# A fused adaLN block, forward and backward: the MLP's inner gradient and its modulated rows transposed from SBUF to SBUF, the filter gradient formed in place

## The chip, the core and the metric

The kernel runs on one core of a Trainium2 chip, in one launch. A core has five instruction queues: TensorE (PE, with its weight loads shown apart as PEld), VectorE (DVE), ScalarE (ACT), GpSimd (POOL) and SyncE (SP). In this kernel SP computes nothing: it issues DMAs, in the order of its queue, and waits in place when the DMA at its head has to wait. The metric is device time in microseconds (us), lower is better; three timed runs of the kernel before gave 420.84, 421.02 and 421.93 us, a median of 421.02 us.

## What is computed

The reference is a forward pass and its vector-Jacobian product. `x` is 2048 rows of 512 channels (S = 2048, D = 512), the MLP has F = 1792 inner channels, everything in bf16:

```python
mod = silu(c) @ w_mod                       # six rows of 512: sa, ca, ga, sb, cb, gb
h = layernorm(x) * (1 + ca) + sa
x = x + ga * irfft2(rfft2(h) * (w_r + 1j * w_i))   # spectral mixing over rows and channels
h = layernorm(x) * (1 + cb) + sb
x = x + gb * (relu(h @ w1 + b1) ** 2 @ w2 + b2)
# outputs: x, and for a given grad_out the gradients of
# A_x, A_w_r, A_w_i, B_w1, B_b1, B_w2, B_b2, c, w_mod
```

Two intermediate quantities matter here. The *modulated rows* are the second `h`, called h2 in the kernel: the MLP's input. The *inner gradient*, gh, is the gradient at the MLP's hidden layer before the ReLU. Then grad w1 = h2ᵀ · gh (a sum over the 2048 rows) and grad b1 is the column sum of gh. For both, TensorE needs gh with rows on the 128 partitions; the kernel produces it with inner channels on the partitions. That is why it has to be transposed. The *filter gradient* is the gradient of w_r and w_i: a complex product of the kept forward spectrum X with the gradient's spectrum G.

## The kernel before

The 2048 rows are 16 tiles of 128 (NT = 16), handled in four batches of four tiles (NB = 4, 512 rows each). The 1792 inner channels are 14 chunks of 128 (NFC = 14). The program is written with a tile framework: pools give out buffers, the framework adds every semaphore wait that a read or a reuse of a buffer needs, and its scheduler orders the instructions of each engine by priorities and its own estimates of durations. [...]

The work goes through these stages:

1. Start: loads, modulation rows, first layer norm, first spectral stage, and `back_products` (line 707), which computes grad_out·w2ᵀ into `gaT[b]`, 14 chunks of [128 channels, 512 rows] per batch. The four `gaT` tiles are a ring of four buffers named `gab` (line 546).
2. The spectral product, forward (`spec_f23`, `spec_g1`).
3. The four batches (line 1025). For batch b, `stage_h(b)` (line 872) computes the hidden layer in pairs of chunks: `r` = ReLU (ACT), `h2` = r·r into a ring of seven buffers, and gh = r·gaT in place in `gaT[b]` (DVE). It stores h to DRAM (line 895) and gh to DRAM (line 896). `stage_o(b)` (line 967) is the MLP's second product, `stage_gn(b)` (line 917) multiplies gh by w1ᵀ and goes back through the layer norm. `stage_m(b+1)` (line 830) forms the modulated rows `h2r`, stores them to DRAM (line 838), and reads them back transposed into `h2T` (line 842), the input of the next `stage_h`. Beside batch 3, `f1_again` (line 997) reloads the gradient rows of batches 0 and 1 from DRAM into tiles named x and y (line 1003) and scales them on DVE (line 1008).
4. `ghn_part(b, fc)` (line 865) reads gh of a finished batch back from DRAM, transposed, two chunks at a time: seven DMAs of 256 KB per batch, into a buffer of the `gab` ring. For batches 0 to 2 these are emitted beside the following batch's `stage_gn`, for batch 3 beside `stage_o(3)`.
5. The backward spectral stage (line 1167): for eight groups, `cmul` forms the product with Z, and with X into `gW` (line 1184), which is stored. Z and X come back from DRAM (lines 1173, 1175; X in a ring of four buffers). Between these, TensorE works off 16 units of `grad_w1` (line 1140), each 16 matmuls of [128, 448], and one `grad_b1` (line 1093): 64 matmuls with 32 output columns, in four column groups of the array that take 448 columns each.
6. The end: the rows' backward pass (`row_pair`, `row_end`) merged with `grad_w2` (line 1224), then the gradient of the modulation.

SP carries nearly all DMAs: the trace has 298 on its queue, 62 of them transposes. Each of its DMAs also waits until the DMA eight places before it has landed, where that is not known from another wait, since eight semaphores are used in turn.

The transposed read of stage 4 is one statement:

```python
nc.sync.dma_start(ghn[b][:, :, fc * P:(fc + 2) * P],
    gh_dram[fc * P:(fc + 2) * P, b * SB:(b + 1) * SB], transpose=True)   # L870
```

## Time and profile before

| what | value |
|---|---|
| median of three timed runs | 421.02 us |
| span of the profiled execution, first to last instruction | 416.3 us |
| what lies around the span, against that median | 4.7 us |
| memory traffic over the span | 35.44 MB read from HBM, 41.60 MB written |
| DMA packets under 512 B | 99049 of 143923 |

The profiled execution's own total is not listed apart from its span, so the difference to the median of the timed runs stands for what lies around it. Two more answers of the trace give the DMAs that the change touches:

| DMA | number | time on SP each (min/median/max) | issue to landing (min/median/max) |
|---|---|---|---|
| store of gh, L896 | 28 | 0.372 / 0.514 / 1.094 us | 3.0 / 3.6 / 5.1 us |
| transposed load of gh, L870 | 28 | 1.277 / 1.309 / 6.002 us | 3.2 / 3.9 / 5.6 us |
| store of the modulated rows, L838 | 8 | 0.332 / 0.344 / 0.349 us | 2.1 / 2.1 / 2.3 us |
| transposed load of the modulated rows, L842 | 6 | 1.237 / 1.238 / 2.003 us | 3.3 / 3.3 / 4.1 us |

"Time on SP" is how long the issuing instruction occupies the queue; "landing" is when the data's semaphore is complete. [...]

### The profile page before, as it was taken

How to read it: one execution, taken by the hardware profiler on the slowest of the kernel's cores; microseconds unless marked ns; L12 is line 12 of the kernel's file. 1: busy time of each engine (PE TensorE's matmuls, PEld its weight loads, DVE VectorE, ACT ScalarE, POOL GpSimd, SP SyncE). 2: the span in 40 equal slices, each digit the busy share in tenths (PEclk: the TensorE clock that was granted, in tenths of full speed). 3: DMA queues.
4: the chain of work that ended last, by engine and by line, in shares of the span. 5: the costliest groups of instructions: out<-in, count | busy, mean ns of one | idle time of the engine just before them, and what ended most of it. 6: DMA issues, size and time to landing. Idle time of an engine off the chain costs nothing. (4 is left out here: it accounts for less than half of the span.)

```text
span 416.3 us, 7175 instructions
## 1 busy us (share of the span) xinstructions
PE 391.7 (94%) x2387; PEld 197.6 (47%) x2407; DVE 343.7 (83%) x827; ACT 277.1 (67%) x495; POOL 60.6 (15%) x147
## 2 busy tenths in 40 slices
PE   2789999999899999999999999999999999999996
PEld 0345445664444444444444444445555665444444
DVE  6899868977988578988897998964999784877885
ACT  4568699868884079338924776545655567897785
POOL 7437950000000000000000000001314520000000
PEclk9999999999999999999999999999999999999999
DMA  8999899979199459949976997998999999999994
GB/s 240 232 261 298 237 213 313 323 239 240 40 331 324 126 161 276 248 128 204 288 227 194 201 291 278 291 213 245 287 280 283 350 265 227 223 269 223 239 266 143
DMA packets 143923, 101.11 MB, mean 243 GB/s; under 512 B 99049, under 2 KB 126830, under 8 KB 143630
## 3 DMA queue, kind: packets, MB, share of 16 engines
q1 hardware_dynamic: 140394, 92.96, 84.1%
q0 software_dynamic: 2784, 7.10, 5.6%
q10 hardware_dynamic: 708, 0.59, 0.5%
q8 instruction: 19, 0.31, 0.3%
q14 instruction: 18, 0.15, 0.1%
HBM read 35.44 MB, written 41.60 MB: 185 GB/s over the span
## 5 line engine op out<-in xcount | busy, mean ns | idle before, releaser
L714 PE MATMUL mm<-gT,w2T 128*128 128x512 bf16 x224 | 57.9, 382 | 4.5 <-ACT gab L719 4.2
L1144 PE MATMUL mm<-gab,h_sb 128*128 128x448 bf16 x256 | 50.9, 352 | 0.0
L1232 PE MATMUL mm<-g_sb,hn 128*128 128x512 bf16 (+1 forms) x250 | 49.6, 352 | 0.8 <-ACT gw L1234 0.4
L915 PE MATMUL og<-w1T,gab 128*128 128x512 bf16 x219 | 49.9, 379 | 0.3
L915 PE MATMUL og<-w,h 128*128 128x512 bf16 x216 | 49.1, 379 | 0.4
L886 PE MATMUL mm<-h2T,w 128*128 128x512 bf16 x164 | 40.2, 379 | 0.5 <-ACT r L888 0.3
L1232 PEld LDWEIGHTS <-hn 128*128 128x128 bf16 x256 | 24.4, 98 | 23.4 <-issue 2.0
L1144 PEld LDWEIGHTS <-h_sb 128*128 128x128 bf16 x256 | 24.6, 98 | 21.8 <-issue 0.8
L886 PEld LDWEIGHTS <-w 128*128 128x128 bf16 x224 | 21.3, 98 | 27.7 <-issue 4.9
L915 PEld LDWEIGHTS <-h 128*128 128x128 bf16 x224 | 21.7, 98 | 25.6 <-DVE h L890 0.6
L915 PEld LDWEIGHTS <-gab 128*128 128x128 bf16 x224 | 21.6, 98 | 25.5 <-DVE gab L894 1.0
L714 PEld LDWEIGHTS <-w2T 128*128 128x128 bf16 x224 | 21.2, 98 | 24.2 <-issue 7.9
L888 ACT ACTIVATE r<-mm,b1col 128x512 bf16<-128x512 f32 x41 | 27.4, 688 | 6.3 <-DVE gab L894 3.3
L294 POOL MEMSET AE<- 128x2 bf16 x4 | 0.3, 103 | 188.5 <-DMA gh_dram<-gab 188.5
L928 ACT CAST G<-og 128x512 bf16<-128x512 f32 x16 | 9.2, 580 | 22.2 <-PE og L915 22.2
L329 ACT ACTIVATE AE<-psB 128x1024 bf16<-128x1024 f32 x16 | 21.8, 1363 | 1.8 <-PE psB L324 0.9
L719 ACT CAST gab<-mm 128x512 bf16<-128x512 f32 x36 | 21.0, 593 | 2.6 <-PE mm L714 2.3
L890 DVE TENSOR_TENSOR h<-r 128x1024 bf16<-128x1024 bf16 x28 | 19.2, 686 | 2.6 <-ACT r L888 2.5
L1148 ACT CAST gw<-mm 128x448 bf16<-128x448 f32 x16 | 8.6, 537 | 18.4 <-PE mm L1144 18.4
L477 DVE SCALAR_TENSOR_TENSOR gm_junk<-wmc,onef,gmbc 128x512 bf16<-128x512 bf16 x24 | 18.0, 750 | 3.3 <-ACT gmbc L467 2.2
L894 DVE TENSOR_TENSOR gab<-r,gab 128x1024 bf16<-128x1024 bf16 x28 | 19.2, 684 | 0.0
L379 ACT ACTIVATE Tsb<-psT 128x512 bf16<-128x512 f32 x32 | 18.5, 603 | 0.6 <-ACT utcs L368 0.5
(292 smaller groups left out, 818.5 us busy)
## 6 DMA issues: line engine op xcount, KB each, us to landing
h_dram<-h SPq DMA_DIRECT2D x28, 256.0 KB, 3.2
gh_dram<-gab SPq DMA_DIRECT2D x28, 256.0 KB, 3.6
w<-in_B_w_dram SPq DMA_DIRECT2D x2, 1792.0 KB, 9.0
wmc<-in_w_mod_dram SPq DMA_DIRECT2D x12, 256.0 KB, 5.8
wz_dram<-Z SPq DMA_DIRECT2D x8, 258.0 KB, 3.8
xs_dram<-Xs SPq DMA_DIRECT2D x8, 258.0 KB, 4.0
Z<-wz_dram SPq DMA_DIRECT2D x8, 258.0 KB, 6.0
Xb<-xs_dram SPq DMA_DIRECT2D x8, 258.0 KB, 8.2
```

The lines of the kernel that those rows point to most:

```text
L329: nc.scalar.activation(dst, ps.rearrange("p r (s e f) -> p (r s) e f", s=2, e=2), AF.Copy, scale=EF_S)
L379: K["Tsb"] = nc.scalar.activation(Tsb, ps, AF.Copy, scale=EF_S).ins
L477: nc.vector.scalar_tensor_tensor(out=junk, in0=wmc[:, i, :], scalar=K["onef"], in1=gmbc, op0=ALU.mult, op1=ALU.mult, accum_out=self.gsc[:, ...
L714: nc.tensor.matmul(ps, lhsT=w2T[:, dc, fc * P:(fc + 1) * P], rhs=gT[b][:, :, dc, :], start=(dc == 0), stop=(dc == 3))
L719: nc.scalar.copy(out=gaT[b][:, fc, :], in_=ps)
L886: nc.tensor.matmul(ps, lhsT=w1[:, dc, (fc + i) * P:(fc + i + 1) * P], rhs=h2T[b][:, :, dc, :], start=(dc == 0), stop=(dc == 3))
L888: nc.scalar.activation(r[:, i, :], ps, AF.Relu, bias=b1col[:, fc + i:fc + i + 1])
L890: nc.vector.tensor_tensor(h2, r, r, op=ALU.mult)
L894: K["gh"] = nc.vector.tensor_tensor(gh, r, gh, op=ALU.mult).ins
L915: nc.tensor.matmul(ps, lhsT=lhs(fc), rhs=rhs[:, fc, :], start=(fc == 0), stop=(fc == NFC - 1))
L1144: nc.tensor.matmul(ps[:, 0:W4], lhsT=h2_sb[:, t, dc * P:(dc + 1) * P], rhs=ghn[t // 4][:, t % 4, fs], start=(t == 0), stop=(t == NT - 1))
L1232: nc.tensor.matmul(ps[:, 0:w], lhsT=hns[fc][:, t, :], rhs=g_sb[:, t, c:c + w], start=(t == 0), stop=(t == NT - 1))
```

## The change

The change has five parts.

1. gh is no longer stored to DRAM. The four `gaT` tiles become one tile `gall` of 4·14 + 2 chunk slots, in which `gaT[b]` starts two slots in. `ghn_part` transposes two chunks of `gaT[b]` into the two slots just before them. So the transposed chunks of a batch take the place of the ones transposed before: chunk pair fc writes the slots that pair fc−2 was read from, and must wait until that transpose has landed and until TensorE has read those slots for the last time in `stage_gn(b)`. The seven transposes of a batch form a chain, and the first pair of a batch follows the last pair of the batch before. The slots 0 and 1 hold two small tiles of the start (`scb`, `srow`) before that.
2. The modulated rows are transposed from `h2r` in SBUF. The store to DRAM stays, since h2 is read again later. The buffer `h2r` (there is one) comes free when both the store and the transpose have landed.
3. The transposed gh now lies block by block (chunk, tile, 128 channels), so `grad_w1` and `grad_b1` take whole chunks: blocks of 4, 3, 4 and 3 chunks, 512 or 384 columns, in place of four times 448. `grad_b1` is read from PSUM by four ACT copies and stored by two DMAs.
4. The filter gradient is written over X. `gW` goes, and X has six buffers in place of four.
5. The last sum of the rows' backward pass is written over `gs`, which has three buffers in place of two; `gx` goes. `gcrow` moves to another pool.

```diff
--- before.py
+++ after.py
@@ -495,7 +495,6 @@
     wz_dram = dram.tile([P, 8, 2, 2, FP], BF16, name="wz_dram")
     xs_dram = dram.tile([P, 8, 2, 2, FP], BF16, name="xs_dram")
     h_dram = dram.tile([NFC, P, NT * P], BF16, name="h_dram")
-    gh_dram = dram.tile([F, NT * P], BF16, name="gh_dram")
     Cd_dram = dram.tile([P, D], BF16, name="Cd_dram")
     LF_dram = dram.tile([P, 16, 3, P], BF16, name="LF_dram")
     LG_dram = dram.tile([P, 16, 3, P], BF16, name="LG_dram")
@@ -543,7 +542,9 @@
     cf_dr = iota_cf(tc, gen)
 
     gap = tc.alloc_tile_pool(name="gap", bufs=1)
-    gaT = [gap.tile([P, NFC, SB], BF16, name="gab", bufs=4) for b in range(NB)]
+    SHIFT = 2
+    gall = gap.tile([P, NB * NFC + SHIFT, SB], BF16, name="gab")
+    gaT = [gall[:, SHIFT + NFC * b:SHIFT + NFC * b + NFC, :] for b in range(NB)]
     w2gp = tc.alloc_tile_pool(name="w2gp", bufs=1)
     zp = tc.alloc_tile_pool(name="zp", bufs=1)
     Z = [zp.tile([P, 2, 2, FP], BF16, name=f"Z{gi}") for gi in range(8)]
@@ -588,7 +589,7 @@
         pv = psM.tile([P, 32], BF16, name="vrow_ps", bufs=1)
         nc.tensor.transpose(pv[:, 0:4 + NFC], vrow, K["ident"][0:4 + NFC, 0:4 + NFC])
         sig = nc.scalar.activation(sigcol, pv[:, 0:4], AF.Sigmoid)
-        scb = p0.tile([P, 4, P], BF16, name="scb")
+        scb = gall[:, 0, :].rearrange("p (a q) -> p a q", q=P)
         for dc in range(4):
             nc.scalar.activation(scb[:, dc, :], pv[:, dc:dc + 1].broadcast_to([P, P]), AF.Copy, scale=sigcol[:, dc:dc + 1])
     nc.vector.tensor_copy(b1col, pv[:, 4:4 + NFC])
@@ -596,7 +597,7 @@
     nc.vector.tensor_copy(scf, scb[:, :, 0])
 
 
-    srow = p0.tile([1, D], BF16, name="srow")
+    srow = gall[0:1, 1, :]
 
     def mod_row(j):
         ps = psM.tile([P, D], FP32, name="mod_ps", bufs=1)
@@ -839,7 +840,7 @@
                 if b > 0:
                     if j == 0:
                         h2T[b] = rows.tile([P, TB, 4, P], BF16, name="h2T", bufs=1)
-                    K["h2T"] = nc.sync.dma_start(h2T[b][:, j:j + 2].rearrange("p j c q -> p (j c) q"), h2_dram[:, t:t + 2, :].rearrange("p j d -> p (j d)"),
+                    K["h2T"] = nc.sync.dma_start(h2T[b][:, j:j + 2].rearrange("p j c q -> p (j c) q"), h2r.rearrange("p j d -> p (j d)"),
                                       transpose=True).ins
 
             return [lambda j=j: one(j) for j in (0, 2)]
@@ -865,9 +866,8 @@
         def ghn_part(b, fc):
 
             if fc == 0:
-                tl = gap.tile([P, NFC, SB], BF16, name="gab", bufs=4)
-                ghn[b] = tl.rearrange("p a b -> p (a b)").rearrange("p (j f) -> p j f", f=F)
-            nc.sync.dma_start(ghn[b][:, :, fc * P:(fc + 2) * P], gh_dram[fc * P:(fc + 2) * P, b * SB:(b + 1) * SB], transpose=True)
+                ghn[b] = gall[:, NFC * b:NFC * b + NFC, :].rearrange("p a (j c) -> p a j c", c=P)
+            nc.sync.dma_start(ghn[b][:, fc:fc + 2].rearrange("p a j c -> p (a j) c"), gaT[b][:, fc:fc + 2, :].rearrange("p a s -> p (a s)"), transpose=True)
 
         def stage_h(b, extra, first):
             sl = slice(b * SB, (b + 1) * SB)
@@ -893,7 +893,6 @@
                 gh = gaT[b][:, fc:fc + 2, :]
                 K["gh"] = nc.vector.tensor_tensor(gh, r, gh, op=ALU.mult).ins
                 nc.sync.dma_start(h_dram[fc:fc + 2, :, sl].rearrange("a p s -> p a s"), h2)
-                nc.sync.dma_start(gh_dram[fc * P:(fc + 2) * P, sl].rearrange("(a p) s -> p a s", p=P), gh)
                 if b == 0 and 0 < fc < 10:
                     load_w1T(fc // 2 - 1)
                 if fc in (4, 10):
@@ -1054,7 +1053,7 @@
                 merge(stage_o(b), [x for p in zip([lambda: None] * 3 + [late_f1.flush] + [lambda: None] * 3, parts) for x in p])
         late.flush()
         nc.vector.tensor_copy(grow[0:96, :], acc[0:96, :])
-        gcrow = constp.tile([1, D], BF16, name="gcrow")
+        gcrow = h2p.tile([1, D], BF16, name="gcrow")
         nc.scalar.copy(out=gcrow, in_=acc[96:97, :])
     hring.release()
     rows.release()
@@ -1080,8 +1079,16 @@
     fin = tc.alloc_tile_pool(name="fin", bufs=2, side="right")
     gmp = tc.alloc_tile_pool(name="gmp", bufs=1, side="right")
     K["LF"] += [lf2.tile([P, 2, 3, P], BF16, name=f"LFb{gi}") for gi in range(4, 8)]
-    W4 = 448
-    NFB = F // W4
+    FBS = [(0, 4), (4, 3), (7, 4), (11, 3)]
+    NFB = len(FBS)
+
+    def gh_rows(t, fb):
+        a, n = FBS[fb]
+        return ghn[t // 4][:, a:a + n, t % 4, :]
+
+    def blocks(ps, fb):
+        return ps[..., 0:FBS[fb][1] * P].rearrange("p (a c) -> p a c", c=P)
+
     gwa = tc.alloc_tile_pool(name="gwa", bufs=1)
     lg2 = tc.alloc_tile_pool(name="lg2", bufs=1)
     K["LG"] = lg2.tile([P, 16, 3, P], BF16, name="LGb")
@@ -1095,11 +1102,15 @@
         ps = mmps.tile([P, SB], FP32, name="mm")
         for t in range(NT):
             for fb in range(NFB):
-                nc.tensor.matmul(ps[32 * fb:32 * fb + 32, 0:W4], lhsT=K["ones_q"], rhs=ghn[t // 4][:, t % 4, fb * W4:(fb + 1) * W4],
+                nc.tensor.matmul(blocks(ps[32 * fb:32 * fb + 32, :], fb), lhsT=K["ones_q"], rhs=gh_rows(t, fb),
                                  start=(t == 0), stop=(t == NT - 1), tile_position=(0, 32 * fb))
-        b4 = gmp.tile([P, W4], BF16, name="b4", bufs=1)
-        nc.scalar.copy(out=b4, in_=ps[:, 0:W4])
-        nc.gpsimd.dma_start(out_5.rearrange("(q f) -> q f", q=NFB), b4[0:P:32, :])
+        b4 = gmp.tile([P, SB], BF16, name="b4", bufs=1)
+        for q in range(4):
+            w = FBS[q][1] * P
+            nc.scalar.copy(out=b4[32 * q:32 * q + 32, 0:w], in_=ps[32 * q:32 * q + 32, 0:w])
+        o5 = out_5.rearrange("(h f) -> h f", h=2)
+        nc.gpsimd.dma_start(o5[:, 0:SB], b4[0:P:64, :])
+        nc.gpsimd.dma_start(o5[:, SB:F // 2], b4[32:P:64, 0:F // 2 - SB])
 
     def add_quadrants(ps, pool, out):
         w = ps.shape[-1]
@@ -1138,16 +1149,16 @@
     w1o = {}
 
     def grad_w1(fb, dc):
-        fs = slice(fb * W4, (fb + 1) * W4)
         ps = mmps.tile([P, SB], FP32, name="mm")
         for t in range(NT):
-            nc.tensor.matmul(ps[:, 0:W4], lhsT=h2_sb[:, t, dc * P:(dc + 1) * P], rhs=ghn[t // 4][:, t % 4, fs],
-                             start=(t == 0), stop=(t == NT - 1))
+            nc.tensor.matmul(blocks(ps, fb), lhsT=h2_sb[:, t, dc * P:(dc + 1) * P], rhs=gh_rows(t, fb), start=(t == 0), stop=(t == NT - 1))
+        a, n = FBS[fb]
         if fb % 2 == 0:
-            w1o[0] = gwa.tile([P, 2, W4], BF16, name="gw1", bufs=3)
-        nc.scalar.copy(out=w1o[0][:, fb % 2, :], in_=ps[:, 0:W4])
+            w1o[0] = gwa.tile([P, F // 2], BF16, name="gw1", bufs=3)
+        half = SB * (fb % 2)
+        nc.scalar.copy(out=w1o[0][:, half:half + n * P], in_=ps[:, 0:n * P])
         if fb % 2 == 1:
-            nc.gpsimd.dma_start(out4_view[:, dc, (fb - 1) * W4:(fb + 1) * W4], w1o[0].rearrange("p a f -> p (a f)"))
+            nc.gpsimd.dma_start(out4_view[:, dc, (a - 4) * P:(a + n) * P], w1o[0])
 
     units = []
     for fp in range(0, NFB, 2):
@@ -1171,7 +1182,7 @@
             if gi >= 4:
                 nc.sync.dma_start(K["LF"][gi], LF_dram[:, 2 * gi:2 * gi + 2])
             nc.sync.dma_start(Z[gi], wz_dram[:, gi])
-            Xt[gi] = fr.tile([P, 2, 2, FP], BF16, name="Xb", bufs=4)
+            Xt[gi] = fr.tile([P, 2, 2, FP], BF16, name="Xb", bufs=6)
             nc.sync.dma_start(Xt[gi], xs_dram[:, gi])
 
         for gi in range(4):
@@ -1181,8 +1192,8 @@
 
         def ew_b(gi, G):
             cmul(nc, ew, Z[gi], G, Z[gi][:, :, 0, 0:DF], Z[gi][:, :, 1, 0:DF], True)
-            gW = ew.tile([P, 2, 2, FP], BF16, name="gW", bufs=3)
-            cmul(nc, ew, Xt[gi], G, gW[:, 0, :, 0:DF], gW[:, 1, :, 0:DF], True)
+            gW = Xt[gi].rearrange("p h i f -> p i h f")
+            cmul(nc, ew, Xt[gi], G, Xt[gi][:, :, 0, 0:DF], Xt[gi][:, :, 1, 0:DF], True)
             for i, o in enumerate((out_2, out_3)):
                 for p0_, n, rows_ in w_parts(o, gi):
                     if gi < 4:
@@ -1297,7 +1308,7 @@
             gh1 = fp.tile([P, 2, D], BF16, name="gh1", bufs=3)
             q1 = fp.tile([P, 2, D], BF16, name="q1", bufs=3)
             gn = fp.tile([P, 2, D], BF16, name="gn")
-            gs = fp.tile([P, 2, D], BF16, name="gs")
+            gs = fp.tile([P, 2, D], BF16, name="gs", bufs=3)
             rr = fp.tile([P, 2, 4], FP32, name="rr")
             for i in range(2):
                 psY = spec_g3(tc, K, Ts[i], psE)
@@ -1320,7 +1331,7 @@
                 for i in range(2):
                     nc.scalar.activation(gn[:, i, :], n1[:, i, :], AF.Identity, scale=rr[:, i, 3:4], bias=rr[:, i, 2:3])
             nc.vector.tensor_tensor(gs, gn, gs, op=ALU.add)
-            gx = fp.tile([P, 2, D], BF16, name="gx")
+            gx = gs
             nc.vector.tensor_tensor(gx, gs, gxl, op=ALU.add)
             nc.sync.dma_start(out1_view[:, t:t + 2, :], gx)
             load_rows3(t + 6)

```

## The prediction

> **What bounds the kernel now.** I read the page's busy shares first, then PE's own waits, then the stretches of 10 us from 120 us on, then SP's queue around the transposes that change.
>
> ```profile
> span 416.3 us, 7175 instructions
> PE 391.7 (94%) x2387; PEld 197.6 (47%) x2407; DVE 343.7 (83%) x827; ACT 277.1 (67%) x495; POOL 60.6 (15%) x147
> ...
> 210.00:220.00 10.00, 9.95 (x47) 4.53 (x47) 9.93 (x26) 3.62 (x6) 0.00 (x0) 1.00 0.80 235
> 240.00:250.00 10.00, 9.89 (x60) 4.23 (x58) 10.00 (x23) 7.49 (x14) 0.15 (x2) 1.00 1.01 297
> 250.00:260.00 10.00, 9.93 (x57) 4.67 (x58) 8.57 (x21) 6.54 (x14) 0.00 (x0) 1.00 0.79 281
> 260.00:270.00 10.00, 9.57 (x55) 4.61 (x55) 9.90 (x25) 4.84 (x10) 0.00 (x0) 1.00 0.95 289
> 270.00:280.00 10.00, 9.46 (x73) 4.42 (x72) 7.67 (x14) 4.28 (x7) 0.00 (x0) 1.00 0.99 222
> 300.00:310.00 10.00, 10.00 (x71) 6.03 (x70) 9.44 (x22) 5.50 (x9) 1.63 (x3) 1.00 0.99 309
> ```
>
> The columns of a stretch are its length, then PE, PEld, DVE, ACT and POOL busy with counts, the granted clock, the DMA share and GB/s. TensorE bounds everything from 120 us to the end. In 210:220 it starts 47 matmuls of 512 columns, one per 213 ns, with no gaps. Over 120:410 its idle time sums to 4.2 us (0.33 in 120:130, 0.97 in 260:280, 1.90 in 340:400, the rest under 0.3 each). None of PE's listed waits after the start names a DMA, except 0.2 us. The DMA engines are near full too, but nobody on the path waits for them. DVE is the second bound in 230:250 and 260:270.
>
> So what a DMA change can give here is capped by 4.2 us, and what it can take is open. The place to look at is SP's queue, because the transposes stand in it and become a chain:
>
> ```profile
> h2T<-h_dram SPq DMA_TRANSPOSE x6, 3.3
> ...
> 230.85 8.45 SPq L870 DMA_TRANSPOSE gab<-gh_dram  x6
> ...
> 245.98 0.64 SPq L1003 DMA_DIRECT2D y<-gx_dram  x1
> ...
> 251.80 1.28 DVE L1008 TENSOR_TENSOR y<-y,modb 128x1024 bf16<-128x1024 bf16 x2
> ...
> 272.31 4.41 SPq L870 DMA_TRANSPOSE gab<-gh_dram  x3
> ...
> 283.20 0.33 SPq L1173 DMA_DIRECT2D Z<-wz_dram  x1
> ...
> 286.15 3.21 PE L1098 MATMUL mm<-gab,ones_q 128*32 128x448 bf16 x64
> ```
>
> Six transposes of batch 2 go out in 8.45 us, back to back, since none waits for another. Behind them stand the gradient rows y, issued at 245.98, which DVE wants at 251.80. The last transposes of batch 3 are issued by 276.7, and grad b1 reads their data in its last quarter, at about 288.
>
> [...]256 KB transposed takes 1.24 us on SP and 3.3 us to land (L842), a plain store of the same size 0.34 and 2.1 us (L838). [...]each step costs a full landing, not an issue. [...] No run here shows a transpose from SBUF.
>
> **The unknown: L, the time from issue to landing of a transpose from SBUF.** Upper neighbour: 3.9 us, the median of the transposes from DRAM, most of which ran beside others. Lower: 2.1 us, the landing of a plain store. A lone transpose from DRAM lands in 3.3 us. [...] I take L = 3.3 us with 1.3 us on SP, since 16 engines write the same 1,024 pieces of 256 B and the chain makes each transpose run alone.
>
> **Part 1, the stores of gh go.** 28 stores x 0.514 us = 14.4 us of SP time and 7.3 MB of writes. SP isn't on the path and PE waits for no DMA: 0 us by itself. 0.2 us of the 0.97 us idle in 260:280 I credit to it.
>
> **Part 1, the chain.** In the changed program's order for batch 2, each transpose waits for the one before, with the stores of h and gx1 between and y behind the last. The second one can go at 227.7: TensorE has then read the first pair for the last time (56 matmuls from 218.13, of which the 44th). Five landings and an issue later, y goes out at 227.7 + 5 x (3.3 + 0.05) + 1.4 = 245.9, against 245.98 now. It lands in some 4.6 us (the row loads' figure), at 250.5, before 251.80. Cost 0, with 1.3 us to spare: the break-even is L = 3.55. Each 0.1 us of L beyond it delays y by 0.5 us. PE's matmuls on y stand in order behind DVE, so a delay is a stall.
>
> For batch 3 the 2 MB load of h2 (issued at 260.49, its packets drained by about 267) lies ahead of the third transpose, which lands at about 268.7. Four more landings with the loads between: 272, 275.6, 279, 284. grad b1 wants the last at 288, and Z's load, behind it on SP, waits for TensorE until 283.2 anyway. Cost 0, 4 us to spare, break-even L near 4.3. The second unit of grad w1 wants chunks 4 to 6 at 285; they are there at 272.
>
> **Part 2, the rows.** h2T no longer waits for the store's landing (SP waited 7.4 us for it in four waits). PE never waited for h2T: 0 us. New: the second `h2r` of a batch waits for the first one's transpose. Issued at about 217.9 it lands at 221.2, and DVE would come to it at 220.6: 0.6 us of stall, with gp, o and x queued behind it. DVE has 1.75 us idle at 223.2, before q, so it is absorbed. [...]
>
> **Part 3, blocks of 512 and 384.** grad w1 keeps its 256 matmuls and 1,792 columns per row tile: 448 columns come at 199 ns each (50.9 us for 256), 512 at 213. Per column that is equal: 0 us. The strided read is like that of L714 (382 ns against 379). grad b1 gets slower: its four column groups run together, and each round lasts as long as its longest. 16 rounds x 64 columns more, at 213 ns per 512: 16 x 27 ns = +0.4 us. Its copy out of PSUM, 0.53 us, becomes four of about 0.5 us each, 1.5 us more on ACT, which idles 2.6 us there: 0.
>
> **Part 4.** The same DVE products, the same stores; two more X buffers let loads go earlier, into stretches where PE is 100% busy: 0 us, -0.1 to +0.3.
>
> **Part 5.** ACT's copies into `gs` no longer wait for DVE's last addition on the buffer, but for a store of three pairs ago. PE idles 1.90 us in 340:400, where this pipeline feeds it. I take a third: -0.7 us, between 0 and -1.9; the scheduler also reorders ACT and DVE there, which could cost 0.5.
>
> **Sum.** +0.4 - 0.7 - 0.2 = -0.5 us: a span of 415.8. The span lies 4.7 us below the median, and nothing outside it changes: 420.5 us. A measurement of this kernel tells about 0.3% (1.3 us) from no change, so this is "same".
>
> **The rivals.**
>
> *Relief.* The stores' traffic costs more than the named waits show: matmuls start later for buffers that come free late. For it: DMA shares near 1 in most stretches, and 14.4 us off SP. Against it: PE's waits name no DMA. If 60% of the 4.2 us go, -2.5 us: 418.5, from 417.2 to 419.7.
>
> *The chain decides (slower).* From L = 3.55 on, y comes late to DVE. At L = 4.5 with 2.5 us on SP, y goes out at 227.7 + 22.75 + 2.5 = 253 and lands at 257.6. That is 5.8 us late, of which DVE's idle 1.4 us in 257:259 absorbs a part: +4.4, and with +0.4 for grad b1, 425.8. Batch 3's chain then still just holds, as TensorE is late too. For it: L = 3.9 is what transposes from DRAM take in company; [...] Against it: a lone one takes 3.3. L = 3.9 makes y 1.7 us late, which is 421.7 to 423[...].
>
> *The transposes from SBUF are made piece by piece.* [...] Nothing in this trace speaks for it.
>
> **How the numbers follow.** Forecast 0.45, range 419.2 to 422.0; relief 0.25; the chain 0.27; piece by piece 0.03. The likeliest is the forecast: 420.5. 417.3 to 429 leaves out about 0.05 below and 0.1 above (the chain's long end and the last case). Faster by over 0.3% (below 419.75): 0.25 from relief, 0.13 of the forecast, 0.38. Within: 0.29 of the forecast and 0.04 of the chain, 0.33. Slower: 0.03 of the forecast, 0.23 of the chain, 0.03: 0.29.
>
> **What would show it.** Landing of the 28 transposes at 3.3 us or less, and 1.3 us each on SP; y issued before 247 and no DVE wait on it; the last transposed chunk landed before grad b1's last quarter. grad b1 at 3.6 us in place of 3.21; less PE idle in 340:400. I am wrong if PE or DVE lists a wait on `gab` or y, if L is above 3.6, or if the span up to 270 us, where TensorE's order is unchanged, moves by more than 1 us.

## The result, and the profile after

The changed kernel is slower: 422.37 us in the median of 20 runs (421.39 to 423.63) against 420.73 for the kernel before beside it, a ratio of 1.0039 with a 95% interval from 1.0026 to 1.0053, or +1.6 us. Run again unchanged on two chips (`f1_after` and `h2_after`) it gave 1.0041 [1.0025, 1.0058] and 1.0047 [1.0027, 1.0067]. The forecast was 420.5 and "same".

The page of the changed kernel, its first lines (busy time, share, instructions):

```profile
span 420.0 us, 7130 instructions
...
PE 392.1 (93%) x2387; PEld 198.0 (47%) x2407; DVE 347.0 (83%) x827; ACT 278.7 (66%) x498; POOL 61.2 (15%) x148
```

TensorE does the same 2387 matmuls in nearly the same time (392.1 us busy, 391.7 before). So the loss is idle time, and the stretches of 10 us say where. The columns are as in the prediction: length, then PE, PEld, DVE, ACT, POOL, clock, DMA share, GB/s.

```profile
240.00:250.00 10.00, 9.89 (x58) 4.24 (x58) 10.00 (x21) 7.70 (x14) 0.14 (x2) 1.00 0.79 208
250.00:260.00 10.00, 8.83 (x55) 4.11 (x53) 8.75 (x21) 5.29 (x12) 0.00 (x0) 1.00 0.99 254
```

In 250:260 TensorE was busy 9.93 us before; now it is 8.83. DVE has 1.25 us without work there, no more than before (1.43), but its pause now lies where TensorE waits for it. First PE's waits in 200:270 (us in all, times, longest), then the product on y in DVE's timeline, then SP's queue (start, time on SP):

```profile
PE psT L277 <- DVE y L258: 1.5, 2, 1.1
```

```profile
254.56 1.29 DVE L1007 TENSOR_TENSOR y<-y,modb 128x1024 bf16<-128x1024 bf16 x2 [1.15 <-PE og L914]
```

```profile
226.86 0.43 SPq L791 DMA_DIRECT2D gb<-in_grad_out_dram  x1
229.14 0.33 SPq L1002 DMA_DIRECT2D x<-gx_dram  x1
229.56 1.24 SPq L870 DMA_TRANSPOSE gab<-gab  x1
...
235.94 4.32 SPq L870 DMA_TRANSPOSE gab<-gab  x2
...
242.15 1.24 SPq L870 DMA_TRANSPOSE gab<-gab  x1
...
245.33 1.25 SPq L870 DMA_TRANSPOSE gab<-gab  x1
...
248.47 1.30 SPq L870 DMA_TRANSPOSE gab<-gab  x1
249.87 0.66 SPq L1002 DMA_DIRECT2D y<-gx_dram  x1
```

The wait of 1.15 us ahead of y is put down to TensorE's `og`, which this product doesn't read; it also waits for y's load, issued at 249.87, and starts 4.7 us after that issue. The load stands behind the chain of transposes, and in the chain one step is long: the transpose issued at 229.56 lets the next one go only at 235.94. The later ones follow each other by 3.1 us. Just ahead of the long one stand two loads of 0.5 MB, gb and x. The records of its packets (1024 of 256 B) begin only at 232.25 and end at 235.27; the loads' packets of 4 KB fill 228 to 233. Over all transposes, however, the median landing is what the forecast took or less (number, median from issue to landing):

```profile
h2T<-h2r SPq DMA_TRANSPOSE x6, 3.1
...
gab<-gab SPq DMA_TRANSPOSE x28, 3.1
```

The kernel before is not free of the wait for y either. Its first profile, from which the prediction read, shows none, but its second one (`h1_before`) does:

```profile
255.31 1.29 DVE L1008 TENSOR_TENSOR y<-y,modb 128x1024 bf16<-128x1024 bf16 x2 [0.21 <-DMA y<-gx_dram]
```

So do its three variants `i1_before_pool`, `g4_before_pool_gs` and `f3_before_pool` (0.42, 0.65 and 0.77 us), where the product starts 5.2 to 6.0 us after y's issue. In the changed kernel the pause is 1.15 to 1.35 us in all four profiles, and the product starts 4.7 to 4.9 us after the issue. So in a usual run there was little to spare at y from the start.

**The two spans must not be subtracted.** 420.0 less 416.3 is 3.7 us, more than twice what the runs show. A second profile of the unchanged kernel before (run `h1_before`) has a span of 420.9. In every listed run the time is 1.8 us above the span, not 4.7, so the first profile belongs to a run of 418.1 us, under the fastest of the 20 timed beside the changed kernel (418.92). Of the 4.5 us between the two profiles, 1.6 arise at the very start, and 3.2 have come together by 100 us. DVE's timeline in the kernel before, first profile:

```profile
3.39 0.22 DVE L102 TENSOR_SCALAR ta_v<-ta_v 128x128 int32<-128x128 int32 x1
```

and in its second profile:

```profile
3.39 3.70 DVE L102 TENSOR_SCALAR ta_v<-ta_v 128x128 int32<-128x128 int32 x1
```

The long form costs TensorE 1.6 us from 12 us on, in either kernel (the start is tested below). So I compare `h1_before` with `h2_after`, the changed kernel profiled beside it on the same chip, which both have the long L102. Their matmuls were matched by the tiles that they read and write, and the difference in start time was read at a few points, whose times are those of the first profile of the kernel before:

| from, to (us) | what lies there | changed minus before, us |
|---|---|---|
| 0, 250 | the first stages | +0.24 |
| 250, 256 | the wait for y, beyond the 0.28 us that `h1_before` loses there | +1.12 |
| 256, 291 | grad b1 +0.42; a wait of 0.67 that this run of the kernel before has | -0.26 |
| 291, 332 | backward spectrum, grad w1 | +0.22 |
| 332, 355 | last spectral products, first rows | +0.15 |
| 355, last matmul | rows and grad w2: -0.44 from the change; -0.34 from a wait of `h1_before` alone | -0.78 |
| last matmul, end | final waits | +0.59 |

The sum is +1.28 for spans of 420.9 and 422.1.

### The profile page after: what moved, and what is told of

It is laid out like the page before. It is cut to its first block, busy times and chain, and to the rows that moved or that the text cites. A ratio compares the mean times of both kernels' runs of the same rounds, so it can differ in the third digit from the quotient of the medians.

```text
span 420.0 us, 7130 instructions
## 1 busy us (share of the span) xinstructions
PE 392.1 (93%) x2387; PEld 198.0 (47%) x2407; DVE 347.0 (83%) x827; ACT 278.7 (66%) x498; POOL 61.2 (15%) x148
## 4 chain that ended last, share of the span: by engine, by line
PE 50%; ACT 17%; DVE 15%; DMA 7%; POOL 4%; issue 3%; SPq 1%; ACTq 0%; POOLq 0%; DVEq 0%
PE og L914 17%; PE mm L1154 8%; PE mm L1243 5%; DMA hn<-h_dram 5%; PE mm L886 5%; PE mm L715 4%; ACT AE L329 2%; PE pst L886 2%; DMA Z<-in_A_w_i_dram 2%; POOL Z L556 2%; PE psG L345 2%; ACT Tsb L379 2%; PE psC L310 2%; ACT gab L720 2%; ACT Xs L312 1%
## 5 line engine op out<-in xcount | busy, mean ns | idle before, releaser
L1154 PE MATMUL mm<-gab,h_sb 128*128 128x512 bf16 (+1 forms) x256 | 51.2, 353 | 0.0
L1159 ACT CAST gw<-mm 128x512 bf16<-128x512 f32 (+1 forms) x16 | 8.6, 538 | 18.6 <-PE mm L1154 18.6
L718 DVE CAST gab<-mm 128x512 bf16<-128x512 f32 x20 | 13.7, 686 | 6.5 <-PE mm L715 6.3
```

Of the source, the lines that this page charges most:

```text
L718: nc.vector.tensor_copy(out=gaT[b][:, fc, :], in_=ps)
L1154: nc.tensor.matmul(blocks(ps, fb), lhsT=h2_sb[:, t, dc * P:(dc + 1) * P], rhs=gh_rows(t, fb), start=(t == 0), stop=(t == NT - 1))
```

## The experiments

Each ratio is against the kernel before, run beside it on the same chip. The groups `e`, `f`, `g` and `h` ran on four chips, `i` on that of `e`. In each group single runs of the kernel before scatter over 5.9 to 8.2 us, so about a microsecond the traces say more than the times.

### Is it y's late reload?

`e1_y_ahead`, and `h3_y_ahead` later as the same kernel. `issue_after` puts an instruction behind another on its queue, without a wait:

```diff
-                nc.sync.dma_start(gxl[b], gx1_dram[:, TB * b:TB * b + TB, :])
+                K["again"] = nc.sync.dma_start(gxl[b], gx1_dram[:, TB * b:TB * b + TB, :]).ins
...
+            def part(fc):
+                with tc.issue_after(K["again"]) if b == NB - 1 and fc >= 10 else ExitStack():
+                    ghn_part(b - 1, fc)
```

> The changed kernel, with the last two transposes of batch 2 put behind the reload of y on SP's queue in place of ahead of it; nothing else moves. Theory S (the loss is y's late reload): y goes out when its buffer comes free, at about 246 us in place of 249.87, DVE's idle 1.15 us ahead of the product on y is gone, TensorE's matmuls on y start 1.1 us earlier against the same matmuls of the kernel before, and the time falls by 1.1 us, from 422.4 to about 421.3. Theory B (the loss is grad b1's longer rounds and what follows it): y goes out earlier too, but the time stays at 422.4. Theory C (reads and writes of the same SBUF by the chain slow the other transfers and engines): 422.4, and y still lands late.

SP's queue and DVE's timeline of `e1_y_ahead`:

```profile
246.13 0.34 SPq L1002 DMA_DIRECT2D y<-gx_dram  x1
246.53 1.31 SPq L870 DMA_TRANSPOSE gab<-gab  x1
```

```profile
253.60 1.31 DVE L1007 TENSOR_TENSOR y<-y,modb 128x1024 bf16<-128x1024 bf16 x2
```

The ratio was 1.0013 [0.9991, 1.0035], which decides between none of the theories.

> The changed kernel with y's reload ahead of the last two transposes of batch 2, nothing else. Theory S: 1.0 to 1.5 us under the changed kernel beside it, 0.2 to 0.7 us above the kernel before. Theory of the start: as the changed kernel within 0.3 us.

`h3_y_ahead` gave 422.63 us, 0.71 under the changed kernel beside it (423.34), ratio 1.0019 [0.9995, 1.0042]. That interval overlaps the changed kernel's; resampling the two sets of 22 listed runs puts the gain at 0.1 to 2.1 us (an estimate). The traces are plainer. The wait for y is gone in both profiles, and the 1.1 us with it: TensorE's lag behind the first profile of the kernel before is the same at 250 and at 256 us (1.82 and 1.82 in `e1`; 2.02 and 2.02 in `h3`), where the changed kernel's grows from 1.53 to 2.75. The time follows only in part. A later wait opens in both profiles (see part 4).

`e2_t_first`: batch 2's first two transposes are emitted ahead of the loads of gb and x, which are then issued after the second.

```diff
+            if b == NB - 1:
+                for done in (2, 4):
+                    ghn_part(b - 1, done - 2)
+            with tc.issue_after(K["ghT"]) if b == NB - 1 else ExitStack():
+                again0, again = f1_again(UT) if b == NB - 1 else ([], [])
...
+            with tc.issue_after(K["ghT" if b == NB - 1 else "h2T"]) if b > 0 else ExitStack():
                 load_rows(b + 1)
```

> The changed kernel, with batch 2's second transpose issued ahead of the two loads of 0.5 MB (gb and x) that stand just before it on SP's queue. Theory S, with the cause of the late y in the loads' packets (the second transpose took 6.4 us to land behind them, the others about 3.1): it lands in 3.5 us or less, the third transpose goes out at about 233 in place of 235.94, y at 246 to 247, DVE's wait ahead of y is under 0.3 us, and the time is about 421.3. If the 6.4 us were a late release by TensorE and not the loads, the third transpose still goes out near 236 and the time stays at 422.4. Theories B and C: 422.4.

SP's queue in `e2_t_first`:

```profile
230.11 1.25 SPq L870 DMA_TRANSPOSE gab<-gab  x1
231.46 0.51 SPq L1002 DMA_DIRECT2D x<-gx_dram  x1
...
233.16 0.42 SPq L791 DMA_DIRECT2D gb<-in_grad_out_dram  x1
233.68 8.82 SPq L870 DMA_TRANSPOSE gab<-gab  x2
...
249.99 0.45 SPq L1002 DMA_DIRECT2D y<-gx_dram  x1
```

The second transpose now lands within 3.6 us, as expected, so the cause is the loads ahead of it and not a late release by TensorE. But the rest of the expectation failed: the third stands behind the loads now, the fourth is issued some 7.5 us after it (the end of the 8.82), and y goes out at 249.99. TensorE loses 0.8 us. The delay goes with the loads to whichever step of the chain is next. Ratio 1.0002 [0.9975, 1.0029].

`e3_gh_dram`: everything as changed, but gh goes through DRAM again, so no transpose has to wait for the one before.

```diff
...
+                nc.sync.dma_start(gh_dram[b, fc // 2], gh.rearrange("p a s -> p (a s)"))
...
-            nc.sync.dma_start(ghn[b][:, fc:fc + 2].rearrange("p a j c -> p (a j) c"), gaT[b][:, fc:fc + 2, :].rearrange("p a s -> p (a s)"), transpose=True)
+            nc.sync.dma_start(ghn[b][:, fc:fc + 2].rearrange("p a j c -> p (a j) c"), gh_dram[b, fc // 2], transpose=True)
```

> The changed kernel, with the inner gradient stored to DRAM and transposed from there again (28 stores of 256 KB more, the same destinations, blocks and buffers as in the changed kernel). No transpose then waits for the landing of the one before. Theory S: the stall of 1.1 us ahead of y goes, grad b1's +0.5 us and the later +0.5 us stay and so does the 0.6 us gained in the row stage: 421.1 to 421.4. Theory B: 422.4, since blocks and later stages are as in the changed kernel. Theory C: 420.7 or less, as nothing reads SBUF by transfer any more. If the stores themselves cost time, as the relief case of the prediction had it: over 422.4.

SP's queue in `e3_gh_dram`:

```profile
230.08 5.60 SPq L871 DMA_TRANSPOSE gab<-gh_dram  x3
...
236.40 4.85 SPq L871 DMA_TRANSPOSE gab<-gh_dram  x3
...
248.44 0.64 SPq L1004 DMA_DIRECT2D y<-gx_dram  x1
```

Six go out in two bunches again, y 1.4 us earlier than in the changed kernel, DVE doesn't wait, TensorE's lag stays at 1.95 us through 250:260. With the same blocks and buffers, the chain that reading from SBUF brings is gone, and the wait for y with it. So the chain makes y late, not the blocks or the buffers. The ratio, 0.9995 [0.9970, 1.0019], adds nothing to that: beside it `e2` and `e4`, in which y stays late, have 1.0002 and 1.0001, so in this group the times don't tell a variant from the kernel before.

### grad b1's blocks

`e4_b1_even`: each of the four column groups takes 64 of the 128 columns of seven chunks, 448 in all; one copy out of PSUM, four small stores.

```diff
-                nc.tensor.matmul(blocks(ps[32 * fb:32 * fb + 32, :], fb), lhsT=K["ones_q"], rhs=gh_rows(t, fb),
...
+                s, h = divmod(q, 2)
+                nc.tensor.matmul(ps[32 * q:32 * q + 32, 0:7 * H].rearrange("p (a c) -> p a c", c=H), lhsT=K["ones_q"],
+                                 rhs=ghn[t // 4][:, 7 * s:7 * s + 7, t % 4, H * h:H * h + H],
```

> The changed kernel, with grad b1 in four equal column groups of 448: each group takes 64 of the 128 columns of seven chunks, and one copy out of PSUM in place of four. Theory B: grad b1 is 0.4 to 0.5 us shorter (its 64 matmuls in 3.2 us, as in the kernel before), and what follows it comes back too: 421.4 to 421.9. Theory S: only grad b1's own 0.4 us comes back: 422.0, and the stall ahead of y stays 1.15 us.

TensorE's timeline of the changed kernel:

```profile
288.67 3.63 PE L1105 MATMUL mm<-gab,ones_q 128*32 128x512 bf16 x64
```

and of `e4_b1_even`:

```profile
289.83 3.21 PE L1107 MATMUL mm<-gab,ones_q 128*32 128x448 bf16 x64
```

The term of +0.4 us is right, and reading 64 columns at a time costs nothing that shows (3.21 us, as in the kernel before). The ratio, 1.0001 [0.9973, 1.0028], doesn't show so small a thing. The stall ahead of y was not 1.15 us as I expected, but 2.1: in this run L102 was short, TensorE was 0.9 us further, and y still went out at 249.81. The stall cost TensorE 3.4 us, since its granted clock fell around the end of it, to 0.50 in 258:260 (see the last section).

`f2_y_b1` has both edits, y ahead and the even groups.

> The changed kernel with two of its costs undone: the last two transposes of batch 2 behind y's reload, and grad b1 in four equal groups. Theory S: no wait ahead of y, grad b1 in 3.2 to 3.3 us, and against the changed kernel in the same call 1.2 to 1.7 us less; that is the time of the kernel before within 0.4 us, or up to 0.3 us under it, for the row stage's gain. Theory T (what is left of the loss lies elsewhere): still 0.7 us or more above the kernel before.

421.51 us, 1.5 under the changed kernel beside it (`f1_after`, 423.02), and 1.0018 [0.9996, 1.0039] of the kernel before. The first half of theory S holds; the remainder of 0.6 us, if it is one, does not fit it. The single runs say where it may lie. Ten of the 22 have a mean granted clock of 0.998 or more and a median of 420.46 us; the other twelve have 0.994 to 0.996 and 422.86. All runs of `f1_after` are at 0.998 or more (423.02), and 70 of 75 of the kernel before (420.82). Sorting runs by what befell them proves no cause, but where the clock held, `f2` is level with the kernel before. Its trace has a wait that the changed kernel hardly has. TensorE's waits in 332:352 of `f2_y_b1`:

```profile
PE psY L387 <- ACT Tsb L379: 1.4, 1, 1.4
PE psT L376 <- ACT utcs L368: 0.4, 1, 0.4
```

### Part 4, the filter gradient in place

The first line of that fence is TensorE waiting at the first row tile for ACT's copy into `Tsb`, whose buffer lies where others were released. In the kernel before, ACT executes 5 semaphore waits ahead of these copies, in all variants with part 4 nine. The copy then waits for a DMA, by the trace the transposed load of `hn` (0.8 us in the changed kernel, 1.9 in `f2_y_b1`, 2.8 in `e1_y_ahead`); `e2` and `e3` are exceptions and name TensorE. What ties the copy to that load was not traced. Besides, the sum behind a product in place starts later on DVE. The kernel before, DVE's timeline, X's last product and the first sum:

```profile
295.98 0.69 DVE L421 TENSOR_TENSOR p<-Xb,G 128x1028 bf16<-128x1028 bf16 x1
296.58 0.43 DVE L422 TENSOR_TENSOR gW<-p 128x514 bf16<-128x514 bf16 x1
```

and the changed kernel:

```profile
298.45 0.69 DVE L421 TENSOR_TENSOR p<-Xb,G 128x1028 bf16<-128x1028 bf16 x1
299.18 0.43 DVE L422 TENSOR_TENSOR Xb<-p 128x514 bf16<-128x514 bf16 x1
```

The sum starts 0.73 us after the product, before it was 0.60. So it is in all seven such pairs of this profile (0.72 to 0.73). Z's sums are in place in both kernels, but another product stands between, and they start 0.61 us after that one. My reading, that the sum waits because it writes over what the product ahead still reads, fits both figures; the cause itself was not shown.

`g1_no_p4` undoes this part alone, and `g2_y_b1_no_p4` on top of `f2_y_b1`:

```diff
-            Xt[gi] = fr.tile([P, 2, 2, FP], BF16, name="Xb", bufs=6)
+            Xt[gi] = fr.tile([P, 2, 2, FP], BF16, name="Xb", bufs=4)
...
-            gW = Xt[gi].rearrange("p h i f -> p i h f")
-            cmul(nc, ew, Xt[gi], G, Xt[gi][:, :, 0, 0:DF], Xt[gi][:, :, 1, 0:DF], True)
+            gW = ew.tile([P, 2, 2, FP], BF16, name="gW", bufs=2)
+            cmul(nc, ew, Xt[gi], G, gW[:, 0, :, 0:DF], gW[:, 1, :, 0:DF], True)
```

> The changed kernel with part 4 undone: the filter gradient again in a buffer of its own (two of them; a third has no room), four X buffers. Theory U (part 4 has a price of its own: each product in place takes 0.13 us longer on DVE, and the first copy into Tsb of the row stage waits for stores out of the X buffers, 1 to 2.3 us of TensorE in five of the eight profiles of variants so far and 0 to 0.3 in the others): no wait of Tsb for a DMA, TensorE's start at psG (L345) no later against the kernel before than at L1154 before it, and 0.3 to 0.8 us under the changed kernel, so 0.8 to 1.3 us above the kernel before. Theory S alone: part 4 costs nothing, +1.6 as the changed kernel. The stall ahead of y stays in both.

> The changed kernel with y's reload ahead of two transposes, grad b1 in equal groups, and part 4 undone: of the change are left the transposes from SBUF, h2T from its row buffer, grad w1 in blocks of 512 and 384, and three gs buffers. Theories S and U together say that nothing else costs time: 0 to 0.6 us under the kernel before, for the row stage; against +0.6 us with part 4 in place. If something else of the change costs, 0.5 us or more above the kernel before.

ACT's waits in 328:352 of `g1_no_p4` name no DMA any more; the last one is as in the kernel before:

```profile
ACT Tsb L379 <- ACT utcs L368: 0.5, 1, 0.5
```

TensorE's lag grows by 0.05 us at L345, in place of 0.3. In `g2`, though, it grows by 0.85 there (TensorE waits for DVE's `utcs`, 0.7 us), so y ahead opens a wait in this variant too. The ratios are 1.0011 [0.9989, 1.0033] and 0.9997 [0.9967, 1.0028]. Both things that theory U names are seen, the later sum (0.73 against 0.60 us) and a DMA ahead of `Tsb` (0.8 us). Their price isn't separable from zero by the times of this chip, and with all three costs undone the kernel can't be told from the kernel before, within 0.3%.

### The start

L102 is long while GpSimd works through its run of small tables (3.2 to 7.0 us). `f3_before_pool` makes the first of them wait for DVE's integer operations, and by order the others (they start at 4.72 us and after, in the kernel before at 3.18):

```diff
-def iotas_lf(tc, g):
+def iotas_lf(tc, g, last):
...
+    with tc.issue_after(last):
+        nc.vector.memset(sm[:, 0, :], 0)
-    nc.gpsimd.iota(sm[:, 0, :], pattern=[[1, 4]], base=0, channel_multiplier=0)
+    first = nc.gpsimd.iota(sm[:, 0, :], pattern=[[1, 4]], base=0, channel_multiplier=0).ins
+    with tc.issue_after(first):
...
-    lf_io = iotas_lf(tc, gen)
+    lf_io = iotas_lf(tc, gen, K["last"])
```

> The kernel before, with GpSimd's small tables at L172 and everything behind them on its queue made to wait for DVE's last integer operation at L130 (one more small memset on DVE carries the wait). If most runs of the kernel before lose the start to GpSimd, as four of five profiles of the changed kernel and its variants did, the time falls by 1.2 to 1.9 us; if about half of them do, by 0.6 to 1.0 us; if the long L102 belongs to the changed kernel, it stays the same within 0.3 us. In its profile L102 takes 0.22 us.

> The changed kernel once more, as the reference for the runs beside it. Theory S: 1.0 to 1.7 us above the kernel before, as in the first comparison (+1.64). Its profile is a second sample of two things that differ from run to run: whether DVE's int32 operation at L102 takes 0.22 or 3.7 us at the start (then TensorE is 1.6 to 1.9 us late from 12 us on), and when y goes out. If y's reload is bound by the transfers and not by TensorE, y goes out at 249.5 to 250.2 us in either case and DVE idles 1 us ahead of it after a late start and 2 us or more after an early one.

`f1_after` had the long L102 again and y out at 250.35. `f3_before_pool` has 0.39 us for L102 and a ratio of 0.9968 [0.9947, 0.9988], 1.0 us under the kernel before. That is what 1.6 us in somewhat more than half of the runs of the kernel before would give.

At that point the long form had shown in six profiles of the changed kernel and its variants (and not in three others) and not in the one of the kernel before, so that the start could itself have been the loss. The `h` runs ask that.

> The kernel before, unchanged, against itself: ratio 1.000 within 0.2%. If the long L102 goes with the program, it takes 0.22 us again; if it is a matter of the run, either. Its span says whether 416.3 us is usual for it: its median run of 420.7 us has a span near 419.

> The changed kernel, unchanged: 1.2 to 1.9 us above the kernel before, L102 at 3.7 us again if that goes with the program, y out at 249.5 to 250.4 us and DVE idle 1.0 to 1.4 us ahead of it.

> The changed kernel with GpSimd's wait at the start, nothing else. Theory S: TensorE is 0.8 to 1.2 us earlier up to 250 us than in the changed kernel, y still goes out near 250 us, DVE's wait ahead of it grows to about 2 us, and the time is that of the changed kernel within 0.4 us. Theory of the start: 0.8 to 1.6 us under the changed kernel, that is the kernel before within 0.5 us.

`h1_before` has the long form too (shown above), with a ratio of 1.0008 [0.9985, 1.0030] to itself: it is a matter of the run, and both kernels pay it. `h4_after_pool` took 422.12 us against `h2_after`'s 423.34 (1.0009 [0.9985, 1.0032] of the kernel before), so the changed kernel gains about what the kernel before gains. The expectation of theory S failed there. Its y went out at 248.77, 3.2 us earlier than in `h2_after`, and the wait ahead of it was 1.34 us in both. So y's lateness is relative to TensorE in most runs, not tied to a fixed time; `e4_b1_even` was the exception.

### A version faster than both

> The changed kernel with both costs undone and with GpSimd's wait at the start. Theory S: 1.2 to 2.0 us under the kernel before in the same call, and under the changed kernel by 2.5 to 3.5 us, if most runs lose the start to GpSimd; y goes out at about 244.5 us and DVE doesn't wait for it. Theory T: no less than the kernel before with that wait alone, plus 0.7 us.

> The same with GpSimd's wait at the start: 0.8 to 1.6 us under the kernel before (the kernel before gained 1.0 us from that wait). If TensorE's earlier arrival is lost again later, at y, at Tsb or at the last loads of h, it is the same as without the wait within 0.4 us.

> The kernel before with GpSimd's wait at the start and part 5 alone (three gs buffers, the last sum in place). Theory S: 1.0 to 1.6 us under the kernel before, as the row stage gave 0.25 to 0.6 us in the profiles of the changed kernel and its variants. If part 5's gain is only made-up time (it follows stalls that come before it), no better than GpSimd's wait alone: 1.0 us under.

> The kernel before with GpSimd's wait at the start, once more: 0.8 to 1.4 us under the kernel before, as in its first run (0.9968).

> The changed kernel with y ahead, equal groups in grad b1, part 4 undone and GpSimd's wait: level with the kernel before plus that wait, within 0.4 us, if what is left of the change is neutral; 0.3 to 0.8 us under it if the row stage's gain shows.

`f4_y_b1_pool` 1.0018 [0.9993, 1.0042]; `g3_y_b1_no_p4_pool` 1.0003 [0.9976, 1.0030] and, as `i2_y_b1_no_p4_pool`, 0.9991 [0.9955, 1.0028]; `g4_before_pool_gs` (the same wait, and `gs` with three buffers, written over) 1.0003 [0.9970, 1.0036]; `i1_before_pool`, which is `f3_before_pool` again, 0.9961 [0.9923, 1.0000]. `i1`'s expectation held; whether `i2` is level with it, as expected, these intervals don't tell. The kernel before with GpSimd's wait is the best, by 0.3 to 0.4%, and nothing of the change adds to it: the expectations of `f4`, `g3` and `g4`, 0.8 to 2.0 us under the kernel before, all failed. `f4` took 422.27 us beside 419.90 of `f3`; in 14 of its 22 runs the mean clock is 0.997 or less (median 423.24), in the other eight the median is 420.46. Part 5 doesn't help on its own. In the one profile of `g4` TensorE waits 4.2 us for ACT's `gs`, three times, in the row stage; whether that is usual, and why, stays open.

## Why the prediction was wrong

**The step that failed** is in "Part 1, the chain": "Five landings and an issue later, y goes out at 227.7 + 5 x (3.3 + 0.05) + 1.4 = 245.9". The structure of the sum was right and the usual landing was if anything shorter than taken, but one of the five landings was mis-sized: the first took 6.4 us and not 3.3. From 229.56 to 249.87 the profile has 6.38 + 4 x 3.13 + 1.40 = 20.31 us, the prediction 18.15. The long term adds 3.03, the four others give 0.87 back. With the start of the chain 0.26 us later than predicted (1.6 us of the shift are the start) y is issued 2.4 us later than predicted. The predicted 1.3 us to spare became a wait of 1.15. The 4.6 us taken for y's own landing held (4.7). The spare time itself was read from one favourable profile: four others of the kernel before and its variants have none. The prediction applied its L to every step, though for batch 3 it let a transpose land behind the 2 MB load of h2. The two loads of 0.5 MB that `load_rows` and `f1_again` put ahead of batch 2's chain were in view and were left out.

Of its signs of being wrong, a wait of DVE on y and y out after 247 us came, an L above 3.6 in the median did not. The rival "the chain decides" named the place, the victims and the order (y, DVE, TensorE) and gave slower. Its threshold, L = 3.55, was stated for a uniform L and not reached in the median (3.1); what decides is the sum over the chain. The long end of that rival and the rival of transposes made piece by piece had no measured number behind them: a transpose from SBUF took 1.24 us on SP in the median of 28, 2.00 at most.

**Stores gone: 0.** Right. They bring nothing on the path. In `e3_gh_dram`, which has them back, TensorE's lag at 250 us (1.95) lies among those of the changed kernel and its variants with a long L102 (1.4 to 3.5). The relief that the rival of that name expected is not seen.

**Part 2: absorbed.** Right: DVE's wait for `h2r` shows as 1.6 us in two waits, with no wait of PE behind it.

**Part 3: +0.4 for grad b1.** Right (3.63 against 3.21): each of the 16 rounds takes 0.20 us before and 0.23 now, little more than one matmul of 448 or of 512 columns (0.199 and 0.213), so the four groups do run together. The 0 for grad w1 held too, 51.2 against 50.9 us busy, though the two figures that it rested on are not equal per column: 199 ns for 448 is 0.44 ns, 213 for 512 is 0.42. The first is a mean of busy time, the second a spacing.

**Part 4: 0 (-0.1 to +0.3).** It left out two costs. The sums in place start about 0.12 us later each, and the first copy into `Tsb` waits for a DMA. In the changed kernel TensorE pays 0.3 us at L345 and 0 to 0.3 at the first row tile. With y ahead the second becomes 1.4 to 2.3 us (`e1`, `h3`, `f2`, `f4`). That the stall ahead of y had covered it is not shown: `h4_after_pool` comes to this place as early as `e1` (lags of 2.8 and 2.9 us) and doesn't wait, and `e4` has both stalls.

**Part 5: -0.7.** Right in sign at most. The lag shrinks by 0.4 to 0.5 us over the rows in the changed kernel's profiles, but TensorE's idle time in 340:400 did not (2.05 us, before 1.91), and `g4`, with part 5 alone, gains nothing.

**"Nothing outside it changes".** 0.6 us was lost after the last matmul. From its start to the end it is 3.44 or 3.45 us in all five profiles of the kernel before and its variants, and 4.03 in the changed kernel's three. In `e3_gh_dram`, with the stores back, it is 3.42; in `g1_no_p4` 3.67, and with equal groups in grad b1 4.2. The last DMA lands 2.1 us after that matmul in every profile. SP then still has semaphores of its DMAs to wait for, one at a time: two in `h1_before`, done at 2.23 us, six in `h2_after`, done at 2.83. These waits make up the 0.6 us, so it matters which place the last DMA's semaphore has among them. No run changed that place alone.

**The account.** In profiles: y +1.1, grad b1 +0.4, in-place sums and the first row about +0.3, the end +0.6, rows -0.4, in sum +2.0 against +1.6 to +2.3 measured (the three medians). The experiments show the first by trace, and `h3` by a time just clear of the noise; grad b1 and the sums in place are shown in traces by undoing them (`e4`, `g1`); the end and the rows are read from traces without an experiment of their own. That the sum fits so well is in part luck, since each size comes from one to four profiles.

## What to carry to other kernels

A chain of transfers is priced step by step: look at what stands on the same queue ahead of each step, because one landing behind a megabyte of loads cost as much here as two (6.4 us against 3.1), and a load that is needed soon is better issued ahead of the chain's last steps (in `e1` y at 246.13 in place of 249.87, and no wait for it). When a stall is removed, look for a wait that opens later before counting the gain. Before two profiles are compared, find out whether each is a typical run: here one operation at the start made 1.6 of the 3.7 us between them, and the spare time at y was in one profile of five.

## What was not expected of the hardware

**Some stalls of about 2 us cost twice.** Around the end of five of TensorE's pauses (0.8 us before it to 1.2 after) the granted clock fell to 0.5, for 3.4 us in four of them and 6.8 in one. Stretches of 2 us in `h3_y_ahead`, after a pause of 1.63 us that ends at 348.4:

```profile
346.00:348.00 2.00, 0.78 (x8) 0.37 (x6) 0.56 (x1) 0.23 (x1) 0.00 (x0) 1.00 1.24 236
348.00:350.00 2.00, 1.58 (x11) 1.15 (x11) 0.00 (x0) 1.95 (x5) 0.48 (x1) 0.65 0.66 67
350.00:352.00 2.00, 2.00 (x7) 0.71 (x5) 0.64 (x2) 1.33 (x3) 0.09 (x1) 0.50 1.05 248
352.00:354.00 2.00, 2.00 (x11) 0.90 (x10) 1.93 (x5) 0.00 (x0) 0.00 (x0) 1.00 1.14 289
```

and in `g4_before_pool_gs`, where a pause of 2.27 us ends at 391.6:

```profile
390.00:392.00 2.00, 0.38 (x1) 0.10 (x1) 0.91 (x2) 2.00 (x5) 0.00 (x0) 1.00 1.09 198
392.00:394.00 2.00, 1.97 (x18) 0.96 (x18) 2.00 (x6) 2.00 (x5) 0.00 (x0) 1.00 1.06 270
```

The clock is the last column but two. At 0.50 matmuls of 512 columns follow each other by 0.43 us in place of 0.21. The five pauses are of 1.63 (`h3`), 1.68 (`g4`), 1.88 (`f4`), 2.03 (`e4`) and 2.26 us (`e1`). Ten others, of 1.17 to 1.51 us, were not followed by it, but neither was the longest, the 2.27 us above. So the length alone does not decide it, and these runs give no threshold. One such drop of 3.4 us takes 0.4% off the mean clock of 420 us, which is the 0.996 that many single runs show. It explains part of why removing y's wait brought less than 1.1 us: the pause at `Tsb` was followed by it in `e1` (2.26 us) and `h3` (1.63), and in `f2` the slower runs are those with the lower clock.

**DVE behind GpSimd.** L102 either takes 0.22 us or lasts as long as GpSimd runs one small table after another, 3.70 us. Of the 13 profiles without the wait of `f3`, nine have the long form and four the short one; the seven with it all have 0.39 us. What decides is not seen: in the two profiles of the kernel before, L102 and the tables ahead of it start within 2 ns of each other. In the long form it lasted over the whole train of GpSimd's instructions (3.18 to 7.0 us), not one of them (0.12 to 0.35 us each). Why it does so, no run here shows.
